# The second head mixing: 112 keys per product on two 64-row halves of the array, in place of 64 and 56 keys on its four quarters

## The chip, the cores and the metric

The kernel runs on one core of a Trainium2 chip. The metric is the device time of one execution in microseconds (us); shorter is better. A core has five engines with queues of their own: TensorE (PE; its weight loads are shown apart as PEld), VectorE (DVE), ScalarE (ACT), GpSimd (POOL) and SyncE (SP, which here only issues DMA transfers). TensorE writes to PSUM, from where ACT and DVE copy results to SBUF.

## The reference

Attention with heads mixed twice ("talking heads"), followed by an MLP with a SiLU, all in float32; batch 4, 12 heads, 448 positions, head width 64, model width 768, hidden width 2048.

```
scores = scale * q @ k^T                          # per batch and head
scores = einsum('bhij,hg->bgij', scores, w_pre)   # first mixing over heads
attn   = softmax(scores)                          # over the keys j
attn   = einsum('bhij,hg->bgij', attn, w_post)    # second mixing over heads
x      = attn @ v                                 # values, then heads side by side
h      = x @ w_in;  g = h * sigmoid(h);  out = g @ w_out
```

## The kernel before

**Two phases.** Up to about 440 us the kernel does the attention; the MLP products (line 624) fill the rest. While the attention runs, the MLP's weights come from float64 words, are converted on DVE, ACT and POOL (lines 63 to 93) and are written back to HBM, so those engines and the DMA queues are shared.

**Groups.** Each batch's 448 query rows are cut into four tiles of 100 to 120 rows. A tile is cut into groups of 10 query rows. A group lies in SBUF as two halves of 64 partitions, each with 60 used rows (5 query rows of 12 heads, row after row), so that mixing over heads is a product with a block-diagonal 60 by 60 matrix on one half of the array. There are 184 groups, worked on in 92 pairs, and the loop over groups takes one pair in two iterations.

**One pair.** `scores` (line 339) makes q k^T for two heads side by side, one on each 64-row half of the array. The copies of it (`st`, lines 344 and 346) are sent by DMA (line 351, SP's queue) into the group layout `g`. `mix_pair` (line 399) does the first mixing of a pair, DVE takes the row maximum (`nm`, line 405), ACT the exponential and its sum (`e`, line 409), POOL and DVE turn the sums into reciprocals (lines 418, 422), and POOL scales the mixing matrix by them (`wr`, line 425). `mix_pair_again` (line 437) is the second mixing. `put_pair` (line 446) copies its result from PSUM (`pa`, one buffer of two banks) to the tile `at` on ACT, and `values` (line 368) multiplies `at` by `v`, for two heads on two 64-column halves of the array. Transposes of q, k (lines 310, 269) stand between them.

**The second mixing in detail.** The exponentials are the stationary operand and `wr` (60 columns) the moving one, so that keys come out on the partitions. The 448 keys are four chunks (`j`) of 112. Each chunk and each row half `s` is cut into a key half `c`: 64 columns of weights for c=0 (56 keys, and 8 more that only fill), 56 for c=1. So the array is used as four 64 by 64 quarters, in the order (0,0), (1,1), (0,1), (1,0), and each quarter writes its own 64 partitions of PSUM; row half `s` has a PSUM bank of its own. A pair is 32 products; a float32 product is issued as two loads of weights and two matrix instructions, so the trace shows 64 of each.

**The values' rows.** `at` and the values have the same gap: 120 partitions, of which rows 56 to 63 are filler. `load_v_quad` (line 251) loads four heads of v in two transfers of 56 rows each (line 259), and where the tile held something else before (the same four tiles serve as space for k, line 240), GpSimd first zeroes rows 32 to 63 (line 256).

**What sets the order.** Each engine takes its instructions in the order in which the program emits them; there is no planner. In an even iteration the loop emits `mix_pair` of a later pair, then the work laid on that iteration in the order prep_q, prep_k, values, scores, then `mix_pair_again`; in an odd iteration such work alone. SP's queue holds the transfers of v, k, q, `st` and the MLP weights in one line. Six `scores` steps for the next tile lie on six successive iterations.

Of the kernel before, what the change touches and what calls it, by code (L numbers as in the profile page):

```python
# [8 lines left out]
F32 = mybir.dt.float32  # L9
# [94 lines left out]
def talking_heads_then_silu_mlp(  # L104
# [11 lines left out]
    nc = tc.nc  # L116
    ctx.enter_context(tc.manual_schedule())
    B, H, S, D = q.shape
# [3 lines left out]
    RH = R // 2  # L122
    GP = 128
    HP = GP // 2
    GH = RH * H
    G0 = HP - GH
    JT = 112
    NJ = S // JT
    JH = JT // 2
    KV = 64 + JH  # L130
    HH = H // 2
    TQ = 12 * R
    LEAD = 4
# [34 lines left out]
    def pool(name, bufs, stack=ctx, **kw):  # L168
        return stack.enter_context(tc.tile_pool(name=name, bufs=bufs, **kw))
# [5 lines left out]
    v2_p = pool("v2", 4, late, side="right")  # L175
    a_p = pool("a", 2, late, side="right")
# [16 lines left out]
    pa = ps_a.tile([128, 2, 512], F32, name="pa", tag="pa")  # L193
    turns = []

    def bank(p, name):
        if p is ps_a:
            turns.append(name)
            return pa[:, len(turns) % 2]
        return p.tile([128, 512], F32, name=name, tag="bank")  # L200

    v_tiles = [v2_p.tile([KV, 4, NJ, D], F32, name="v4", tag="v4") for _ in range(4)]
    zeroed = []
    g_tiles = [p.tile([GP, 12, S], F32, name="g", tag="g") for p in g_ps]

    def load_weights():
# [31 lines left out]
    def load_k_pair(b, h, queues=(nc.sync, nc.sync)):  # L238
        if h >= 4 if b == 0 else h // 4 != 1:
            x = (b * H + 8) // 4 % 4 if b else h // 4 - 1  # L240
            if x in zeroed:
                zeroed.remove(x)
            t = v_tiles[x][:JT, h % 4:h % 4 + 2].rearrange("p i j d -> p (i j d)")
            t = t.rearrange("p (j i d) -> p j i d", i=2, j=NJ)
        else:
            t = nat.tile([JT, NJ, 2, D], F32, name="kn", tag="kn")
        kns[b, h] = t
        for i in range(2):
            queues[i].dma_start(out=t[:, :, i, :], in_=k[b, h + i].rearrange("(p j) d -> p j d", p=JT))

    def load_v_quad(b, h):
        x = (b * H + h + 8) // 4 % 4
        t = v_tiles[x]
        if x not in zeroed:
            zeroed.append(x)
            nc.gpsimd.memset(t[32:64], 0.0)
        src = v[b, h:h + 4].rearrange("i (c p j) d -> c p i j d", c=2, p=JH)
        for c in (1, 0):
            nc.sync.dma_start(out=t[64 * c:64 * c + JH], in_=src[c])
        for i in range(0, 4, 2):  # L260
            vs[b, h + i] = t[:, i:i + 2]

# [117 lines left out]
    class Group:  # L380
# [48 lines left out]
        def mix_pair_again(self, other):  # L429

            for x, g in enumerate((self, other)):
                half = pa[:, :, x * 256:x * 256 + NJ * GH]
                for j in range(NJ):
                    for s, c in ((0, 0), (1, 1), (0, 1), (1, 0)):
                        rows = slice(HP * s, HP * (s + 1))
                        m = JH if c else 64
                        nc.tensor.matmul(  # L437
                            half[64 * c:64 * c + m, s, j * GH:(j + 1) * GH],
                            lhsT=g.e[rows, j * JT + c * JH:j * JT + c * JH + m], rhs=g.wr[rows], start=True, stop=True)

        def put_pair(self):
            if self.slot == 0:
                ats[self.n] = a_p.tile([KV, NJ, H, TQ], F32, name="at", tag="at")
            o, np, p = self.place()
            o += 2 * p * R
            nc.scalar.copy(  # L446
                out=ats[self.n].rearrange("p j g t -> p (j g) t")[:, :, o:o + 2 * R].rearrange("p x (c i) -> p x c i", i=RH),
                in_=pa[:KV].rearrange("p s (g w) -> p (s g) w", g=2)[:, :, :NJ * GH].rearrange("p c (x i) -> p x c i", i=RH))

    seq = [(b, ti) for b in range(B) for ti in range(len(tiles))]  # L450
    kns, qns, ks, vs, qs, gs, ats = {}, {}, {}, {}, {}, {}, {}
# [9 lines left out]
    at = lambda i: groups[i] if 0 <= i < len(groups) else None  # L461
# [13 lines left out]
    for n in range(1, len(seq)):  # L475
        p0, p1 = first[n - 1], first[n]
        spread = (0, 0, 0, 0, 2, 2) if n == 1 else (-6, -5, -4, -2, -1, 0) if p1 - p0 == 12 else (-6, -5, -4, -3, -2, -1)
        for h in range(0 if n > 1 else 2 * NE, H, 2):
            i = p0 + spread[h // 2]
# [7 lines left out]
    for n, (b, ti) in enumerate(seq):  # L487
        if n:
            p0 = first[n - 1]
            if n > 2:  # L490
                put(first[n - 2], lambda n=n: load_q(n)[0](), lead=7, w=2.1)
            for hg, i in ((0, p0 - 9), (1, p0 - 8)):
                if n > 1:
                    put(i, prep_q, n, hg)
            if ti == 0:
                c0 = first[n - 2]
                for h, i, lead in zip(range(0, H, 2), (0, 1, 3, 5, 7, 9), (10, 10, 11, 12, 5, 6)):
                    put(c0 + i, load_k_pair, b, h, lead=lead, w=1.2)
                    put(c0 + i, prep_k, b, h)
        if ti == 0:  # L500
            for h in range(0, H, 4):
                put(first[n] + ((5, 6, 8) if n else (15, 16, 18))[h // 4], load_v_quad, b, h, lead=2, w=1.8)
# [23 lines left out]
    for h in range(0, 6, 2):  # L526
        load_k_pair(0, h, (nc.sync, nc.scalar))
    loads[1]()
    for h in range(6, H, 2):
        load_k_pair(0, h)  # L530
# [58 lines left out]
    for j in range(WB, len(parts)):  # L589
        kind, m = ("i", "o")[j // (7 * NP)], j // NP % 7  # L590
        kind0, m0, p0 = ("i", "o")[(j - WB) // (7 * NP)], (j - WB) // NP % 7, (j - WB) % NP
        n = HC if kind0 == "i" else HF
        s = step_of[kind0, m0, NU - 1, (4 * p0 + 3) // n] + 1
        s = max(s, step_of[kind, m, 0, 0] - (10 if kind == "i" or m == 0 else 3))
# [52 lines left out]
    for kind, n, nk, blocks in (("i", HF, HC, xs), ("o", HC, HF, gr)):  # L647
        for m in range(7):
            for u in range(NU):
                s = step_of[kind, m, u, 0]  # L650
# [5 lines left out]
        for d, (x, y, z) in enumerate(DIFFER):  # L656
            for u in range(NU):
                s = step_of[kind, d, u, 0] if kind == "o" or d > 1 else step_of[kind, 0, u, 0]
# [8 lines left out]
    for i in range(len(groups) + 1):  # L667
        g, new, old = at(i), at(i + LEAD), at(i - 1)
# [182 lines left out]
    for s, (kind, m, u, a) in enumerate(steps):  # L851
# [14 lines left out]
        p = None  # L866
        if s >= len(phs):
            p = bank(ps_h, "ph")
# [58 lines left out]
```

## Time and profile before

| | |
|---|---|
| median of 3 runs | 872.0 us (870.98, 872.0, 878.78) |
| the profiled execution | 876.44 us, span 874.7 us from the first to the last instruction |
| mean granted TensorE clock | 0.977 of full speed |
| TensorE, matrix instructions | 828.4 us busy, 11058 instructions |
| TensorE, weight loads | 656.0 us, 11058 instructions |
| DVE, ACT, POOL | 625.4, 526.5, 406.4 us busy |

Busy time of an engine counts each moment once, though instructions overlap; a matrix instruction's duration holds its way through the array, so that neighbours overlap in time. Lines are written L437 for line 437. In the chain of waits, the work that ended last is followed back from the last instruction to whatever released it, so each microsecond of the span is put down to one line. "Idle before" in square brackets is the time for which the engine stood still ahead of the row, and what ended it. Shapes such as 64*56 are rows by columns of the array in use.

### The profile page before, as it was taken

What the parts mean: (1) busy time and instruction counts of PE and PEld (TensorE: products, weight loads), DVE (VectorE), ACT (ScalarE), POOL (GpSimd) and SP (SyncE); (2) the same over time, 40 slices, a digit from 0 to 9 for tenths busy, and PEclk for the clock granted to TensorE, in tenths of its full rate; (3) what the DMA queues carried; (4) which work ended last, traced back from release to release, by engine and by line L of the source; (5) the groups of instructions that cost most, each with busy time, mean ns of one, the idle gap of its engine ahead of it and who ended that gap; (6) DMA issues with size and microseconds to landing.
All of it is one profiled execution on the core that took longest, in us unless ns stands there. A gap on an engine that the chain in (4) does not pass through costs nothing.

```text
span 874.7 us, 27490 instructions
## 1 busy us (share of the span) xinstructions
PE 828.4 (95%) x11058; PEld 656.0 (75%) x11058; DVE 625.4 (71%) x1218; ACT 526.5 (60%) x1178; POOL 406.4 (46%) x681
## 2 busy tenths in 40 slices
PE   7797999899998999899899999999999999999997
PEld 5355666567666666666599999988899889999986
DVE  5453777468775777675878899999988689984332
ACT  4575778578786878677756653324694245343242
POOL 6231445355454645463877577557742233133020
PEclk7999899899999999999999999999999999999999
DMA  7569677887788787874635453355331142112234
GB/s 143 167 182 193 185 212 218 219 216 196 209 242 229 220 219 211 228 214 151 188 104 184 144 167 118 118 151 155 107 94 49 35 114 71 38 49 73 73 85 106
DMA packets 162343, 132.89 MB, mean 152 GB/s; under 512 B 50409, under 2 KB 155861, under 8 KB 162215
## 3 DMA queue, kind: packets, MB, share of 16 engines
q1 hardware_dynamic: 158809, 129.39, 53.0%
q8 instruction: 87, 1.43, 0.7%
q0 software_dynamic: 544, 1.03, 0.5%
q10 hardware_dynamic: 2862, 0.71, 0.4%
q14 instruction: 41, 0.34, 0.1%
HBM read 64.01 MB, written 27.53 MB: 105 GB/s over the span
## 4 chain that ended last, share of the span: by engine, by line
PE 75%; DVE 9%; DMA 7%; ACT 4%; issue 2%; SPq 2%; POOL 1%; ACTq 0%; POOLq 0%; DVEq 0%
PE ph L624 41%; PE pa L437 8%; PE pp L399 8%; PE po L368 7%; PE pqk L339 7%; DMA g<-st 4%; ACT e L409 2%; DVE nm L405 1%; DVE g L824 1%; PE pt L269 1%; PE ptt L844 1%; ACT at L446 1%; DVE op L630 1%; DMA v<-in_v 1%; DVE cg L92 1%
## 5 line engine op out<-in xcount | busy, mean ns | idle before, releaser
L624 PE MATMUL ph<-op,wh 128*128 128x448 f32 x924 | 221.5, 368 | 2.4 <-DVE g L834 1.8
L610 POOL TENSOR_TENSOR wl<-wl,wh 128x512 fp32r<-128x512 f32 x84 | 122.0, 1467 | 152.8 <-ACT wh L609 152.3
L624 PEld LDWEIGHTS ph<-op,wh 128*128 128x128 f32 x924 | 171.6, 188 | 18.1 <-DVE g L834 2.1
L405 DVE TENSOR_REDUCE nm<-pp 128x1 f32<-128x448 f32 x184 | 106.1, 618 | 76.1 <-PE pp L399 75.7
L425 POOL TENSOR_SCALAR wr<-wpost,r 128x60 f32<-128x60 f32 x184 | 70.7, 397 | 177.5 <-DVE r L422 139.0
L409 ACT ACTIVATE e<-pp,nm 128x448 f32<-128x448 f32 x184 | 115.4, 631 | 51.1 <-DVE nm L405 48.8
L437 PEld LDWEIGHTS pa<-wr,e 64*64 64x64 f32 (+1 forms) x5888 | 96.7, 131 | 44.9 <-issue 26.5
L437 PE MATMUL pa<-wr,e 64*64 64x60 f32 (+1 forms) x5888 | 108.6, 219 | 14.4 <-ACT at L446 8.6
L624 PE MATMUL ph<-op,wl 128*128 128x448 f32 x462 | 118.9, 366 | 0.0
L399 PE MATMUL pp<-g,wpre 64*64 64x448 f32 x736 | 104.9, 591 | 9.6 <-ACT e L409 5.7
L66 POOL TENSOR_TENSOR cg<-cw,cg 128x256 f32<-128x256 f32 x96 | 75.8, 790 | 76.6 <-DVE cw L63 73.5
L624 PEld LDWEIGHTS ph<-op,wl 128*128 128x128 f32 x462 | 86.7, 188 | 7.5 <-POOL wl L610 0.5
L446 ACT COPY at<-pa 120x960 f32<-120x960 f32 x92 | 89.9, 978 | 3.2 <-PE pa L437 3.2
L368 PE MATMUL po<-at,v 120*64 120x120 f32 (+1 forms) x1536 | 88.1, 268 | 1.8 <-DMA v<-in_v 1.5
L368 PEld LDWEIGHTS po<-at,v 120*64 120x64 f32 x1536 | 77.4, 139 | 14.6 <-issue 5.1
L609 ACT CAST wh<-wl 128x512 fp32r<-128x512 f32 x84 | 51.1, 617 | 54.3 <-DMA wl<-wo_dram 27.2
L344 DVE COPY st<-pqk 120x448 f32<-120x448 f32 (+1 forms) x89 | 55.0, 618 | 36.5 <-PE pqk L339 17.5
L90 ACT ACTIVATE cg<-cg,ebias 128x256 int32<-128x256 int32 x96 | 49.6, 516 | 44.2 <-DVE cg L86 43.0
L92 DVE SCALAR_TENSOR_TENSOR cg<-cw,cg 128x256 int32<-128x256 int32 x96 | 56.2, 586 | 16.4 <-ACT cg L90 16.0
L624 PE MATMUL ph<-x,wh 128*128 128x448 f32 x252 | 64.7, 365 | 0.0
L339 PEld LDWEIGHTS pqk<-kh,qh 64*120 64x120 f32 (+1 forms) x186 | 19.0, 179 | 50.0 <-issue 17.7
L339 PE MATMUL pqk<-kh,qh 64*120 64x448 f32 (+1 forms) x186 | 47.6, 467 | 6.8 <-ACT st L346 5.4
(122 smaller groups left out, 1379.0 us busy)
## 6 DMA issues: line engine op xcount, KB each, us to landing
g<-st SPq DMA_DIRECT2D x132, 210.0 KB
cw<-in_moe_w_in SPq DMA_DIRECT2D x48, 256.0 KB
cw<-in_moe_w_out SPq DMA_DIRECT2D x48, 256.0 KB
wi_dram<-cg SPq DMA_DIRECT2D x24, 448.0 KB
wo_dram<-cg SPq DMA_DIRECT2D x24, 448.0 KB
wl<-wi_dram SPq DMA_DIRECT2D x42, 256.0 KB
wl<-wo_dram SPq DMA_DIRECT2D x42, 256.0 KB
g<-st SPq DMA_DIRECT2D x48, 175.0 KB
```

Of the source, the lines that this page charges most:

```text
L66: nc.gpsimd.tensor_mul(out=e, in0=m, in1=e)
L92: nc.vector.scalar_tensor_tensor(out=e, in0=hi, scalar=-2 ** 31, in1=e, op0=ALU.bitwise_and, op1=ALU.bitwise_or)
L339: nc.tensor.matmul(ps[i][:m, :S], lhsT=q_[rows, hh, :m], rhs=k_[rows], start=(step == 0), stop=(step == 2))
L368: nc.tensor.matmul(po[i * D:(i + 1) * D, c * m:(c + 1) * m], lhsT=vs[b, h][:, i, j, :], rhs=ats[n][:, j, h + i, :m], start=(j == 0), stop= ...
L399: nc.tensor.matmul((self, other)[r].p[HP * c:HP * (c + 1), :S], lhsT=wpre[rows], rhs=gs[self.n][rows, o // R + c * np + p, :], start=True, ...
L405: nc.vector.tensor_reduce(out=self.nm, in_=self.p[:GP, :S], axis=AX.X, op=ALU.max, negate=True)
L409: nc.scalar.activation(out=self.e, in_=self.p[:GP, :S], func=AF.Exp, bias=self.nm, scale=1.0, accum_out=sums)
L425: nc.gpsimd.tensor_scalar(out=g.wr, in0=wpost.rearrange("p g i -> p (g i)"), scalar1=r[:, i:i + 1], scalar2=1.0, op0=ALU.mult, op1=ALU.mult)
L437: nc.tensor.matmul(half[64 * c:64 * c + m, s, j * GH:(j + 1) * GH], lhsT=g.e[rows, j * JT + c * JH:j * JT + c * JH + m], rhs=g.wr[rows], s ...
L446: nc.scalar.copy(out=ats[self.n].rearrange("p j g t -> p (j g) t")[:, :, o:o + 2 * R].rearrange("p x (c i) -> p x c i", i=RH), in_=pa[:KV] ...
L610: nc.gpsimd.tensor_sub(out=wl, in0=raw(wl), in1=raw(wh))
L624: nc.tensor.matmul(p[:, :T], lhsT=w, rhs=x, start=(n == 0), stop=(n == len(todo) - 1))
```

## The change

`mix_pair_again` no longer cuts a chunk of 112 keys in two: each row half takes all 112 as one stationary operand, so that the array is used as two halves of 64 rows by 128 columns, and a pair is 16 products (32 loads and 32 matrix instructions). With that the gap in `at` and in the values goes: both are 112 partitions, v comes in one transfer of 112 rows per four heads (12 transfers, not 24), and the zeroing on GpSimd and the list that records it are taken out. The order of keys, the moving operand, the copy's free shape and the order of the steps are as before.

```diff
-    v_tiles = [v2_p.tile([KV, 4, NJ, D], F32, name="v4", tag="v4") for _ in range(4)]
-    zeroed = []
+    v_tiles = [v2_p.tile([JT, 4, NJ, D], F32, name="v4", tag="v4") for _ in range(4)]
...
-        if x not in zeroed:
-            zeroed.append(x)
-            nc.gpsimd.memset(t[32:64], 0.0)
-        src = v[b, h:h + 4].rearrange("i (c p j) d -> c p i j d", c=2, p=JH)
-        for c in (1, 0):
-            nc.sync.dma_start(out=t[64 * c:64 * c + JH], in_=src[c])
+        nc.sync.dma_start(out=t, in_=v[b, h:h + 4].rearrange("i (p j) d -> p i j d", p=JT))
...
                 for j in range(NJ):
-                    for s, c in ((0, 0), (1, 1), (0, 1), (1, 0)):
+                    for s in range(2):
                         rows = slice(HP * s, HP * (s + 1))
-                        m = JH if c else 64
                         nc.tensor.matmul(
-                            half[64 * c:64 * c + m, s, j * GH:(j + 1) * GH],
-                            lhsT=g.e[rows, j * JT + c * JH:j * JT + c * JH + m], rhs=g.wr[rows], start=True, stop=True)
+                            half[:JT, s, j * GH:(j + 1) * GH], lhsT=g.e[rows, j * JT:(j + 1) * JT], rhs=g.wr[rows],
+                            start=True, stop=True)
...
-                ats[self.n] = a_p.tile([KV, NJ, H, TQ], F32, name="at", tag="at")
+                ats[self.n] = a_p.tile([JT, NJ, H, TQ], F32, name="at", tag="at")
...
-                in_=pa[:KV].rearrange("p s (g w) -> p (s g) w", g=2)[:, :, :NJ * GH].rearrange("p c (x i) -> p x c i", i=RH))
+                in_=pa[:JT].rearrange("p s (g w) -> p (s g) w", g=2)[:, :, :NJ * GH].rearrange("p c (x i) -> p x c i", i=RH))
```

## Rows read from the trace of the kernel before

**Rows 1.** The page's busy time: engine, us (share of the span), instructions.
```profile
PE 828.4 (95%) x11058; PEld 656.0 (75%) x11058; DVE 625.4 (71%) x1218; ACT 526.5 (60%) x1178; POOL 406.4 (46%) x681
```

**Rows 2.** Windows: from:to, length, busy (count) per engine, clock, DMA share, GB/s.
```profile
34.00:438.00 404.00, 375.25 (x8707) 250.25 (x8706) 270.58 (x644) 306.75 (x742) 192.88 (x454) 0.97 0.75 206
...
18.00:24.80 6.80, 5.41 (x42) 3.44 (x38) 4.54 (x10) 4.71 (x8) 6.80 (x7) 1.00 0.58 158
...
300.00:312.00 12.00, 11.54 (x240) 8.06 (x239) 9.17 (x22) 10.11 (x24) 6.16 (x16) 1.00 0.93 239
```

**Rows 3.** Chain of waits: shares of the span by line, then pieces (start, us, what).
```profile
by line: PE ph L624 41.4%; PE pa L437 8.2%; PE pp L399 7.6%; PE po L368 7.2%; PE pqk L339 6.9%; DMA g<-st 3.9%; issue 2.1%; ACT e L409 1.5%; DVE nm L405 1.4%; DVE g L824 1.3%; PE pt L269 1.3%; PE ptt L844 1.0%; ACT at L446 1.0%; DVE op L630
...
117.49 1.09 PE pa L437 x58
...
159.97 9.64 DMA g<-st
```

**Rows 4.** Timeline, 300 to 312 us: start, us, engine, line, operation, count [idle before].
```profile
301.28 1.63 PEld L368 LDWEIGHTS po<-at,v 120*64 120x64 f32 x32 [0.70 <-ACT kh L274]
301.28 1.86 PE L368 MATMUL po<-at,v 120*64 120x120 f32 x32
...
303.07 1.02 PEld L437 LDWEIGHTS pa<-wr,e 64*64 64x64 f32 x64 [0.16 <-issue]
303.07 1.16 PE L437 MATMUL pa<-wr,e 64*64 64x60 f32 x64
...
304.16 0.53 PE L310 MATMUL pt<-ident,qn 120*128 120x120 f32 x3
...
304.52 0.55 PE L269 MATMUL pt<-ident,kn 112*128 112x112 f32 x4
...
305.00 0.98 PE L399 MATMUL pp<-g,wpre 64*64 64x448 f32 x8
...
306.91 1.16 PE L437 MATMUL pa<-wr,e 64*64 64x60 f32 x64 [0.46 <-ACT at L446]
```

**Rows 5.** Groups by line and form: count | busy us, mean ns | idle before.
```profile
L437 PE MATMUL pa<-wr,e 64*64 64x60 f32 x2944 | 108.6, 222 | 14.2 <-ACT at L446 8.6 <-issue 3.4 <-POOL cg L66 1.3
...
L437 PE MATMUL pa<-wr,e 64*56 64x60 f32 x2944 | 98.7, 217 | 0.2 <-issue 0.2
...
L437 PEld LDWEIGHTS pa<-wr,e 64*64 64x64 f32 x2944 | 96.7, 135 | 44.9 <-issue 26.5 <-POOL r L418 5.2 <-POOL cg L66 4.3
...
L437 PEld LDWEIGHTS pa<-wr,e 64*56 64x56 f32 x2944 | 86.0, 127 | 0.0
```

**Rows 6.** Timeline, 18 to 25 us: weight loads, then matrix instructions.
```profile
18.14 0.18 PEld L339 LDWEIGHTS pqk<-kl,qh 64*120 64x120 f32 x2
18.34 0.18 PEld L339 LDWEIGHTS pqk<-kh,qh 64*120 64x120 f32 x2
...
24.05 0.52 PEld L516 LDWEIGHTS pa<-ident 128*128 128x128 f32 x4 [0.32 <-DVE st L344]
...
18.14 0.36 PE L339 MATMUL pqk<-kh,ql 64*120 64x448 f32 x2
18.34 0.37 PE L339 MATMUL pqk<-kl,qh 64*120 64x448 f32 x2
```

**Rows 7.** Timeline of TensorE, 52 to 58 us: what stands beside the second mixing.
```profile
52.56 1.16 PE L437 MATMUL pa<-wr,e 64*64 64x60 f32 x64
53.53 1.42 PE L399 MATMUL pp<-g,wpre 64*64 64x448 f32 x8
...
55.19 0.37 PE L339 MATMUL pqk<-kh,ql 64*120 64x448 f32 x2
55.39 0.37 PE L339 MATMUL pqk<-kl,qh 64*120 64x448 f32 x2
55.69 1.16 PE L437 MATMUL pa<-wr,e 64*64 64x60 f32 x64
56.78 0.46 PE L339 MATMUL pqk<-kh,qh 64*120 64x448 f32 x2
```

**Rows 8.** The values' line: each operation's count and ns (min/median/max), first and last start.
```profile
L259 SPq DMA_DIRECT2D v<-in_v x24: 316/594/4061, 61.0 to 361.7; - x24
L256 POOL MEMSET v<- x6: 942/942/946, 60.9 to 352.4; 32x1024 f32 x6
```

**Rows 9.** Waits of SP's queue, 34 to 440 us: us in total, times, longest.
```profile
SPq L259 <- POOL r L418: 5.5, 5, 1.8
```

**Rows 10.** Timeline, 60 to 92 us: a stall of TensorE in the first batch.
```profile
87.89 0.69 PE L339 MATMUL pqk<-kh,qh 64*100 64x448 f32 x1 [4.54 <-ACT st L346]
```

More of the change, by code (lines that the diff above doesn't have):

```diff
@@ L128, in talking_heads_then_silu_mlp @@
     NJ = S // JT
-    JH = JT // 2
-    KV = 64 + JH
     HH = H // 2
@@ L240, in load_k_pair @@
             x = (b * H + 8) // 4 % 4 if b else h // 4 - 1
-            if x in zeroed:
-                zeroed.remove(x)
-            t = v_tiles[x][:JT, h % 4:h % 4 + 2].rearrange("p i j d -> p (i j d)")
+            t = v_tiles[x][:, h % 4:h % 4 + 2].rearrange("p i j d -> p (i j d)")
             t = t.rearrange("p (j i d) -> p j i d", i=2, j=NJ)
```

## Prediction

> **What bounds the kernel now.** I read the busy times first: TensorE's matrix instructions fill 95% of the span, DVE, the next engine, 71% [rows 1]. That is a hint only, since their durations overlap; so next I read the attention phase as a window, because the change touches nothing after it. There TensorE is busy 375.25 of 404 us at a mean clock of 0.97, ACT 306.75, DVE 270.58 [rows 2]. TensorE stands still for 28.75 us in all, and that is the slack that could hide longer work. Third, the chain of waits: the second mixing (L437) alone holds 8.2% of the span, 0.082 x 874.7 = 71.7 us; a whole burst of it stands on the chain with 1.09 us [rows 3], so some 71.7 / 1.09 = 66 of the 92 bursts lie on the path that sets the end. Fourth, the timeline of one iteration shows why: values, second mixing, transposes and first mixing follow on TensorE with no gap between them (301.28 to 305.98 us), and the next burst waits only 0.46 us, for the copy L446, which itself waited in ACT's queue behind work fed by TensorE [rows 4]. Whatever lengthens a burst there lengthens the iteration.
>
> **What sets the pace of a burst.** This is the step on which all hangs. A burst has 64 loads of weights in 1.02 us [rows 4]; four quarters work side by side, so each does 16 in a row. The loads of 64 and of 56 columns occur equally often with the same 60 moving columns, and yet those of 64 take 96.7 us together and those of 56 take 86.0 [rows 5]: a ratio of 1.124, against 64/56 = 1.143. So the columns loaded set the pace of the 64-column quarters, not the moving columns, and not the count. One round (one load on every quarter) takes (1.02 - 0.14) / 15 = 0.0587 us, with 0.14 for the last load's own duration. The only row with full-width loads at full clock and a short moving operand is the 128-column product of L516: four loads in 0.52 us, each about 0.19, so (0.52 - 0.19) / 3 = 0.110 us a round [rows 6]. Both stretches had the clock of 1.00 of full speed, that is 2.4 GHz [rows 2]. The straight line through 64 and 128 columns gives 0.0008 us per column, and for 112 columns 0.0587 + 48 x 0.0008 = 0.0971 us.
>
> Do two 64-row loads run side by side? In the scores, which use the array just as the change will (64 rows, 120 columns), two loads together take the 0.18 us that one takes, and the matrix instructions of two successive steps begin 0.20 us apart though their 448 columns alone are most of that [rows 6]; so the halves load at once, and a load hides under the matrix instruction ahead of it.
>
> **The change part by part.** *The burst.* Sixteen rounds stay sixteen: four chunks, two groups, two instructions a product. Before, a round was four loads of at most 64 columns; now it is two of 112. Half the instructions go, no round goes, and each becomes 0.0971 - 0.0587 = 0.0384 us longer: 16 x 0.0384 = 0.614 us per burst, from 1.09 to about 1.70 us. The bounds are the nearest rows: 0.0587 (a round stays as it is, +0) and 0.110 (a 128-column round, 16 x 0.0513 = +0.82 us). I take the value between, since 112 lies nearer to 128. The trace of the scores shows the 120-column load with 0.18 us against 0.135 for 64 columns [rows 5, 6], the same slope. The Trainium skill ("TensorE: Matmul & The Clock Gate", section LDWEIGHTS) says that a load takes its columns divided by 1.2 GHz, whatever the rows; by that a round would go from 53 to 93 ns, a burst would grow by 0.64 us and the first term below would be 42 us, so the rule speaks against this change as the rows do.
>
> On the chain: 66 x 0.614 = +40.5 us. The 26 other bursts grow by 16 us in all, where TensorE waits for something else, as in the stalls of 4.54 us for a copy [rows 10] and 9.64 us for a transfer [rows 3]. Their cover is the 28.75 us of idle time; but only idle time right behind a burst helps, so I count a quarter, +4 (bounds 0 and +16).
>
> *The array's shape at a burst's edges.* From the second to the first mixing, both on quarters, the next instruction starts 0.97 us after the burst's start; where scores follow, 1.09: 0.12 us is paid for the change of shape. Ahead of a burst, scores to scores take 0.20 us and scores to burst 0.30 [rows 7]. Now the burst has the scores' shape: edges with scores get up to 0.10 us cheaper, edges with the first mixing up to 0.12 dearer; others stay. By the order of emission scores stand right ahead of the burst in about half of the pairs, 45 of 92, and behind it in fewer. Bounds: 90 x 0.10 = -9, and 47 x 0.12 = +6; I take -4.
>
> *Loads of v and the zeroing.* Six zeroings of 0.94 us go from POOL, and 12 of 24 issues, median 0.594 us, from SP; the bytes stay [rows 8]. POOL is 46% busy [rows 1], so its 5.7 us buy little by themselves. On SP's one line a v transfer that waits for POOL holds up the scores' transfers behind it: 5.5 us in five waits [rows 9]. If all of that were cover for nothing else, -6; if the waits are for a reader of the tile and stay, 0; a doubled transfer that lands later for the values is excluded as a loss beyond 2 us, since values need both parts anyhow. I take -2.
>
> *At no cost.* The ACT copy keeps its 960 elements per partition, the values keep their 64 columns loaded and 120 moved; 112 rows instead of 120 change neither count [rows 4]. If row count mattered, it would be a gain of at most a fifteenth of either.
>
> *The sum.* 40.5 + 4 - 4 - 2 = +38.5 us. Against the profiled execution that is 876.4 + 38.5 = 914.9; that execution stands 4.4 us above the median of the runs, 872.0, so I forecast 910 us.
>
> **The rivals.** *A, faster: the number of instructions sets the pace.* Place: the 128 instructions of a burst at TensorE's front end. A load and matrix pair starts every 1.02 / 64 = 0.016 us; if that were the limit, 32 pairs would take half, the burst would fall by 0.5 us, the chain by 66 x 0.5 = 33, and with -6 for the edges and v the time would be 833. It decides if two wide loads cost less than four narrow ones, that is if a round stays under 0.0587. For it: half the instructions do go. Against it: the 64-column loads are slower than the 56-column ones at equal counts [rows 5]. The Trainium skill ("TensorEngine Tiling (Array Packing)", section Instruction Overhead) gives each matmul about 60 cycles of overhead, by which the moving 60 columns would be at the floor and the count would rule, as in this rival; the trace does not agree, as 64 matrix instructions in 1.16 us are 18 ns each. Chance 0.07.
>
> *B, the slack takes most of it.* If the 28.75 us of idle time lie right behind bursts, 16 + 40.5 - 28.75 = +28, and with the shape and v at their best ends (-9 and -6) +13: 885. For it: stalls do occur in the attention; against: they follow transfers and copies that TensorE's own earlier scores feed, so they move along. Chance 0.08 for 880 to 893.
>
> *C, a round stays 0.0587.* Then nothing but the edges and v remain: -6, 866, within 1%. For it: the lower bound of the burst; against it: L516's 0.110. Chance 0.05.
>
> *D, the loads stop hiding.* If in the new shape a load waits for its half's matrix instruction, a round is 0.0971 plus some 0.05 for the 60 moving columns (half of the 0.10 that 120 take in the values: 1.63 / 32 x 2 halves [rows 4]): +0.0384 + 0.05 = 0.088 x 16 = 1.41 us, 66 times: +93, 959. Against it: the scores' 0.20 us spacing [rows 6]. Chance 0.04.
>
> **How the numbers follow.** The forecast, 893 to 930, has chance 0.76: its lower end is the sum with v and edges at -15 and no help lost off the chain (+26), its upper end all 92 bursts at 0.614 (56) plus 2. The range reaches down to B's lower part, 885, and up to 930; that holds 0.8. What a measurement of this kernel can tell from no change is about 1%, 863 to 881: C's place. Faster 0.07 (A), within 1% 0.06 (C and the edge of B), slower 0.87.
>
> **What would show it.** In the changed trace: bursts of L437 with 32 loads in about 1.5 us and 1.6 to 1.7 us on the chain; loads of 112 columns near 0.175 us each; L437's share of the chain near 112 of 915 us; starts of burst and scores 0.1 us closer. Wrong: 32 loads in 0.5 us (A) or 1.0 (C) or 2.3 (D); or bursts that grow while TensorE's idle time in the attention falls by as much (B).

## The result: slower by 1.4%, a third of the forecast

The changed kernel takes 889.27 us (median of 6 runs, 883.32 to 890.92) where the kernel before, in the same session, takes 877.66 (870.98 to 887.74): ratio 1.0138, 95% interval 1.01 to 1.0175, which is +12 us. Two more sets of runs of the changed kernel gave 1.0155 (1.01 to 1.021) and 1.0148 (1.0103 to 1.0193). Forecast were +38 us and 910 us: the right sign, three times the size. The profiled execution took 885.52 us, with a span of 883.8.

The page of the changed kernel, busy times and the queue that brings instructions (packets, MB, share). The lines have moved by about ten: the second mixing is L426, its copy L435, first mixing L389, scores L329, values L358.

```profile
PE 856.3 (97%) x8114; PEld 708.8 (80%) x8114; DVE 625.1 (71%) x1218; ACT 527.8 (60%) x1178; POOL 401.5 (45%) x675
...
q8 instruction: 64, 1.05, 0.5%
```

Its timeline around one burst (compare [rows 4]), TensorE's loads and matrix instructions:

```profile
302.49 1.65 PEld L426 LDWEIGHTS pa<-wr,e 64*112 64x112 f32 x32 [0.16 <-issue]
...
302.49 1.79 PE L426 MATMUL pa<-wr,e 64*112 64x60 f32 x32
304.21 0.53 PE L300 MATMUL pt<-ident,qn 120*128 120x120 f32 x3
```

The burst did what was forecast: 16 rounds in 1.65 us, of which the last load is 0.175 (the mean of these loads on the page is 175 ns), so (1.65 - 0.175) / 15 = 0.098 us a round against a forecast of 0.0971. From the burst's start to the next instruction it takes 1.72 us (before 1.09). At the scores it is less, as this timeline of the changed kernel shows (compare [rows 7]):

```profile
50.60 0.37 PE L329 MATMUL pqk<-kl,qh 64*120 64x448 f32 x2
50.80 1.69 PE L426 MATMUL pa<-wr,e 64*112 64x60 f32 x32
52.42 0.98 PE L389 MATMUL pp<-g,wpre 64*64 64x448 f32 x8
...
54.05 1.69 PE L426 MATMUL pa<-wr,e 64*112 64x60 f32 x32
55.55 0.45 PE L329 MATMUL pqk<-kh,qh 64*120 64x448 f32 x2
```

Scores to burst take 0.20 us (before 0.30), burst to scores 1.50, burst to first mixing 1.62: the 0.12 us for a change of shape has gone over from one neighbour to the other.

So the cost came; something else gave most of it back. The windows of the changed kernel show where, with busy times per engine, the granted clock and the DMA share:

```profile
34.00:438.00 404.00, 392.93 (x5626) 294.11 (x5625) 264.30 (x633) 300.96 (x724) 181.51 (x437) 1.00 0.73 202
...
68.00:100.00 32.00, 30.67 (x440) 23.08 (x438) 18.59 (x44) 22.45 (x55) 9.61 (x25) 1.00 0.90 222
...
140.00:180.00 40.00, 39.23 (x594) 29.70 (x592) 25.96 (x66) 30.07 (x75) 18.69 (x47) 1.00 0.85 215
```

And the last two for the kernel before, with a short piece inside each:

```profile
68.00:100.00 32.00, 27.18 (x547) 17.98 (x547) 14.31 (x35) 18.50 (x46) 6.93 (x19) 0.89 0.84 190
140.00:180.00 40.00, 35.06 (x793) 22.72 (x789) 23.96 (x59) 27.83 (x66) 18.28 (x43) 0.91 0.84 226
...
88.00:92.00 4.00, 4.00 (x19) 1.65 (x19) 2.34 (x6) 1.96 (x5) 0.74 (x1) 0.50 0.78 211
...
172.00:175.00 3.00, 3.00 (x18) 1.28 (x19) 1.51 (x4) 1.71 (x5) 0.49 (x2) 0.50 0.64 230
```

TensorE's idle time in the attention fell from 28.75 us [rows 2] to 404 - 392.93 = 11.07. And its clock stands at full speed for longer. In the kernel before it was at half (1.2 GHz) around the stalls (0.50 from 88 to 92 and from 172 to 175 us), which makes 0.89 and 0.91 of these two stretches. From the first burst to the last, the trace of the kernel before has 23.9 us at half clock, in 20.7 of which TensorE worked; that of the changed kernel has 3.4, with 3.3 of work. A burst and a first mixing in such a piece of the kernel before, right behind waits for the scores' copies:

```profile
168.13 1.94 PE L437 MATMUL pa<-wr,e 64*64 64x60 f32 x64
171.72 2.38 PE L399 MATMUL pp<-g,wpre 64*64 64x448 f32 x8 [1.65 <-ACT e L409]
```

They take 1.94 and 2.38 us where [rows 4] have 1.16 and 0.98. Which waits went is read from TensorE's waits in 34 to 438 us (us in total, times, longest). Before:

```profile
PE pa L437 <- ACT at L446: 8.6, 17, 1.1
PE pp L399 <- ACT e L409: 5.7, 6, 1.7
PE pqk L339 <- ACT st L346: 5.4, 2, 4.5
PE pa L437 <- issue: 3.6, 3, 2.0
PE po L368 <- DMA v<-in_v: 1.5, 1, 1.5
PE pqk L339 <- DVE st L344: 1.4, 2, 1.1
PE pa L437 <- POOL cg L66: 1.3, 1, 1.3
...
PE po L368 <- issue: 0.3, 1, 0.3
```

After, in full:

```profile
PE pa L426 <- ACT at L435: 7.8, 18, 1.1
PE pt L300 <- ACT st L336: 1.2, 1, 1.2
PE pqk L329 <- ACT st L336: 0.9, 1, 0.9
PE pa L426 <- POOL cg L71: 0.6, 1, 0.6
```

The wait for the burst's own copy stays; the waits for exponentials, for the scores' copies, for v and for nothing visible ("issue") nearly vanish. The chain of waits of the changed kernel says the same (compare [rows 3]):

```profile
by line: PE ph L613 39.4%; PE pa L426 14.5%; PE po L358 8.3%; PE pp L389 7.6%; PE pqk L329 7.3%; DMA g<-st 1.6%; issue 1.6%; SPq L244 1.3%; ACT at L435 1.3%; DVE g L813 1.3%; PE ptt L833 1.0%; DVE op L619 1.0%; DVE g L815 1.0%; DVE cg L92 1
```

The second mixing's part grew from 71.7 to 0.145 x 883.8 = 128 us, the scores' transfers fell from 34 to 14.

**The account.** From the first burst to the last instruction of the last one, TensorE's time can be cut at the start of each group of like instructions, idle time apart. Summed from the two traces, in us, before to after: second mixing 101.8 to 151.0 (+49.2), scores 74.1 to 65.0 (-9.1), first mixing 94.0 to 85.4 (-8.6), values 80.7 to 78.3 (-2.4), transposes 23.2 to 22.8 (-0.4), idle 28.7 to 11.5 (-17.2): +11.5 in all. Of the -20.5 us of the four middle terms, some 6 are edges: about 60 of them, from scores to a burst, at 0.10 us. Some 8 are clock, if work at half clock takes twice its time (18.9 us of work outside the bursts stood at half clock before, 3.3 after). The other 6 or 7 are neither. Most of that is in the first mixing: 12 of them took over 1.0 us at full clock in the kernel before (1.42 us at 53.53 in [rows 7]), 4 in the changed kernel, where 0.91 is usual. These are probably short waits for the exponentials, hidden under the recorded durations; no run shows it apart. (The span grew by 9.1 us. The first burst began at 29.8 us and not at 34.2, before anything that the change touches, as it did in some of the quarter kernels below; behind the last burst the changed kernel took 2 us more.)

One profile of each kernel is compared here. In the two other profiles of the changed kernel (taken with experiments 2 and 5) the same sum is +14.6 and +15.6 us, the idle time 13.0 and 14.3 us, and the time at half clock 10.2 us in each, so single terms are good to 3 or 4 us.

### The profile page after: what moved, and what is told of

It is laid out like the page before. It is cut to its first block, busy times and chain, and to the rows that moved or that the text cites. A ratio compares the mean times of both kernels' runs of the same rounds, so it can differ in the third digit from the quotient of the medians.

```text
span 883.8 us, 21565 instructions
## 1 busy us (share of the span) xinstructions
PE 856.3 (97%) x8114; PEld 708.8 (80%) x8114; DVE 625.1 (71%) x1218; ACT 527.8 (60%) x1178; POOL 401.5 (45%) x675
## 4 chain that ended last, share of the span: by engine, by line
PE 80%; DVE 9%; ACT 3%; DMA 3%; SPq 2%; issue 2%; POOL 0%; ACTq 0%; DVEq 0%; POOLq 0%
PE ph L613 39%; PE pa L426 14%; PE po L358 8%; PE pp L389 8%; PE pqk L329 7%; DMA g<-st 2%; SPq L244 1%; ACT at L435 1%; DVE g L813 1%; PE ptt L833 1%; DVE op L619 1%; DVE g L815 1%; DVE cg L92 1%; PE pt L259 1%; ACT e L399 1%
## 5 line engine op out<-in xcount | busy, mean ns | idle before, releaser
L426 PEld LDWEIGHTS pa<-wr,e 64*112 64x112 f32 x2944 | 157.4, 175 | 25.9 <-issue 12.0
L426 PE MATMUL pa<-wr,e 64*112 64x60 f32 x2944 | 160.6, 258 | 9.1 <-ACT at L435 8.2
L389 PE MATMUL pp<-g,wpre 64*64 64x448 f32 x736 | 95.3, 571 | 0.8 <-ACT e L399 0.5
L435 ACT COPY at<-pa 112x960 f32<-112x960 f32 x92 | 89.6, 974 | 5.8 <-PE pa L426 5.8
L358 PE MATMUL po<-at,v 112*64 112x120 f32 (+1 forms) x1536 | 85.7, 265 | 0.0
L358 PEld LDWEIGHTS po<-at,v 112*64 112x64 f32 x1536 | 75.5, 137 | 11.0 <-issue 5.2
L329 PEld LDWEIGHTS pqk<-kh,qh 64*120 64x120 f32 (+1 forms) x186 | 18.8, 176 | 40.9 <-issue 21.5
L336 ACT COPY st<-pqk 120x448 f32<-120x448 f32 (+1 forms) x89 | 47.9, 539 | 4.2 <-DMA g<-st 3.1
```

Of the source, the lines that this page charges most:

```text
L329: nc.tensor.matmul(ps[i][:m, :S], lhsT=q_[rows, hh, :m], rhs=k_[rows], start=(step == 0), stop=(step == 2))
L358: nc.tensor.matmul(po[i * D:(i + 1) * D, c * m:(c + 1) * m], lhsT=vs[b, h][:, i, j, :], rhs=ats[n][:, j, h + i, :m], start=(j == 0), stop= ...
L389: nc.tensor.matmul((self, other)[r].p[HP * c:HP * (c + 1), :S], lhsT=wpre[rows], rhs=gs[self.n][rows, o // R + c * np + p, :], start=True, ...
L426: nc.tensor.matmul(half[:JT, s, j * GH:(j + 1) * GH], lhsT=g.e[rows, j * JT:(j + 1) * JT], rhs=g.wr[rows], start=True, stop=True)
L435: nc.scalar.copy(out=ats[self.n].rearrange("p j g t -> p (j g) t")[:, :, o:o + 2 * R].rearrange("p x (c i) -> p x c i", i=RH), in_=pa[:JT] ...
```

## Experiments

Each kernel was timed in five rounds against the kernel before. Theory S: longer bursts take the place of idle and slow-clock time that TensorE had anyway. Theory V: the new loads of v removed the stalls. Theory I, formed after experiments 1 to 3: half the instructions relieve TensorE's supply of instructions.

**1. The new loads of v alone.** On top of the changed kernel, the mixing goes back to quarters, cut so that no gap is needed:

```diff
-                    for s in range(2):
+                    for s, c in ((0, 0), (1, 1), (0, 1), (1, 0)):
...
+                        m = JT - 64 if c else 64
...
+                            half[64 * c:64 * c + m, s, j * GH:(j + 1) * GH],
+                            lhsT=g.e[rows, j * JT + c * 64:j * JT + c * 64 + m], rhs=g.wr[rows], start=True, stop=True)
```

> The new loads of v (112 rows, one transfer, no zeroing) with the mixing back on four quarters, cut into 64 and 48 keys, so that there is no gap either. The round should stay at 0.0587 us, as the 64-column quarters set it, and the burst at 1.09 us. Theory V (the new loads of v took TensorE's stalls away, and the wide loads cost what was forecast): 15 to 25 us faster than the kernel before, some 855 to 862 us, with TensorE's idle time in the attention near 10 us. Theory S (the longer bursts filled idle time that was there anyway, and v matters little): within 5 us of the kernel before, idle time of TensorE in the attention still 20 to 30 us.

Measured: ratio 0.9985 (0.9953 to 1.0017), TensorE idle for 404 - 375.07 = 28.9 us in 34 to 438 us:

```profile
34.00:438.00 404.00, 375.07 (x8696) 251.87 (x8689) 269.42 (x643) 306.47 (x739) 188.65 (x449) 0.97 0.75 207
```

TensorE stands still as long as in the kernel before, though not for the same waits alone (more for "issue", see experiment 3). Theory V falls: v's transfers and the zeroing are worth nothing that can be told from zero on the quarters.

**2. The wide mixing with the old loads of v.** The changed kernel with two transfers of 56 rows and a zeroing:

```diff
...
-        nc.sync.dma_start(out=t, in_=v[b, h:h + 4].rearrange("i (p j) d -> p i j d", p=JT))
+        if x not in zeroed:
+            zeroed.append(x)
+            nc.gpsimd.memset(t[32:56], 0.0)
+        src = v[b, h:h + 4].rearrange("i (c p j) d -> c p i j d", c=2, p=JT // 2)
+        for c in (1, 0):
+            nc.sync.dma_start(out=t[56 * c:56 * c + 56], in_=src[c])
```

> The changed kernel's mixing on two halves with v loaded as before: two transfers of 56 rows per quad, and a zeroing on GpSimd (24 rows, at the same places in the order) that the second transfer waits for. Theory V: 15 to 25 us slower than the changed kernel, 900 to 912 us, with stalls of TensorE back. Theory S: within 4 us of the changed kernel (889 us), idle time of TensorE in the attention 9 to 14 us.

Measured: 1.0205 (1.0147 to 1.0263), idle 404 - 391.43 = 12.6 us:

```profile
34.00:438.00 404.00, 391.43 (x5489) 292.45 (x5486) 256.39 (x612) 294.29 (x707) 178.73 (x427) 0.98 0.72 196
```

It was run again beside the changed kernel:

> The changed kernel's mixing with the old loads of v once more, now beside the changed kernel on the same chip. If the loads of v matter (theory V, in a small form): 4 to 8 us slower than the changed kernel beside it. If not: within 3 us of it.

> The changed kernel, as the yardstick for the run with the old loads of v: 1.010 to 1.018 of the kernel before.

Measured: 1.0181 (1.0134 to 1.0229) against 1.0148 (1.0103 to 1.0193), medians 893.50 and 887.53 us. The idle time stays low with the old loads too. The loads of v may be worth 3 to 6 us on the halves, but the intervals overlap; the forecast's -2 us is neither shown nor refuted.

**3. Longer bursts on the quarters, with more instructions.** The kernel before mixes two of the four chunks twice (8 more rounds), or one (4 more, with `(0,)`):

```diff
-                for j in range(NJ):
+                for j in (*range(NJ), *(0, 1)):
```

> The kernel before with chunks 0 and 1 of every group mixed twice (the same values written again): 8 more rounds on four quarters, 8 x 0.0587 = 0.47 us per burst and 43 us in all, close to the 45.5 us by which the bursts grew in the changed kernel; loads of v and the array's shape as before. Theory S: the same fate as the change, +12 to +22 us (no cheaper edges beside the scores), TensorE's idle time in the attention down from 29 to 10 to 15 us and its mean clock there up to 1.00. Theory V: +35 to +43 us, the stalls still there.

> The kernel before with chunk 0 of every group mixed twice: 4 more rounds, 0.235 us per burst, 21.6 us in all. Theory S: most of it goes into idle time and into the clock, 0 to +8 us, so that the second 21.6 us (the run with 8 more rounds) cost more than the first. Theory V, or any theory in which TensorE's time on the chain simply adds: +15 to +21 us, half of the run with 8 more rounds.

Measured: 1.0578 (1.0503 to 1.0654) for 8 rounds, +51 us; 1.0306 (1.0264 to 1.0347) for 4, +27 us. Both above the TensorE time added (43 and 21.6), where theory S wanted a third of it, and with 8 rounds TensorE's idle time in 34 to 438 us rose, to 404 - 370.07 = 33.9 us. The trace of the kernel with 8 more rounds shows a wait that is rare before. Its timeline of TensorE:

```profile
193.05 0.47 PE L368 MATMUL po<-at,v 120*64 120x120 f32 x5
195.33 0.88 PE L368 MATMUL po<-at,v 120*64 120x120 f32 x13 [1.81 <-issue]
196.14 0.98 PE L399 MATMUL pp<-g,wpre 64*64 64x448 f32 x8
197.05 0.45 PE L339 MATMUL pqk<-kh,qh 64*100 64x448 f32 x2
197.34 0.36 PE L339 MATMUL pqk<-kh,ql 64*100 64x448 f32 x2
197.54 0.37 PE L339 MATMUL pqk<-kl,qh 64*100 64x448 f32 x2
197.83 1.62 PE L437 MATMUL pa<-wr,e 64*64 64x60 f32 x96
199.39 0.45 PE L339 MATMUL pqk<-kh,qh 64*100 64x448 f32 x2
199.67 0.37 PE L339 MATMUL pqk<-kh,ql 64*100 64x448 f32 x2
202.63 0.44 PE L339 MATMUL pqk<-kl,qh 64*100 64x448 f32 x2 [2.59 <-issue]
```

TensorE stops in the middle of `values` and in the middle of a step of the scores, where no other engine is waited for, and between the two stops lie 13 + 8 + 2 + 2 + 2 + 96 + 2 + 2 = 127 matrix instructions, with their loads 254. The page's instruction queue has for this kernel

```profile
q8 instruction: 110, 1.80, 0.9%
```

so a packet carries 1.80 MB / 110 = 16.4 KB, and 2 x 14002 instructions of TensorE over 110 packets make 255 each. The stops stand one packet apart: TensorE had used up its instructions and waited for the next packet. In this kernel's trace the stops of over 0.6 us from 130 to 400 us, 15 of them, all stand at the same place of a packet (counted in the instructions of TensorE's queue, its waits on semaphores included, the remainder by 256 is 193 or 194), and each ends 1.3 to 1.7 us after a packet's transfer ended. The waits put down to "issue", kernel with 8 more rounds:

```profile
PE pa L437 <- issue: 10.4, 9, 3.8
PE pqk L339 <- issue: 9.0, 6, 2.6
PE po L368 <- issue: 5.5, 3, 2.7
PE pt L310 <- issue: 0.9, 1, 0.9
PE pp L399 <- issue: 0.2, 1, 0.2
```

That is 26.0 us (21.6 with 4 more rounds, 3.9 in the kernel before, 10.4 and 9.0 in the quarter kernels of experiments 1 and 6, 7.0, 5.0 and 1.8 in those of experiment 4 with 141, 282 and 448 columns, none in any profile of the mixing with 112 columns).

**4. Longer bursts with few instructions.** To part the time from the instructions, four products with many moving columns stand ahead of each burst of the kernel before, written to the same PSUM tile and overwritten by it:

```diff
+            for s, c in ((0, 0), (1, 1), (0, 1), (1, 0)):
+                rows = slice(HP * s, HP * (s + 1))
+                nc.tensor.matmul(
+                    pa[HP * c:HP * (c + 1), s, :282], lhsT=wpre[rows], rhs=self.e[rows, :282], start=True, stop=True)
```

> The kernel before with 4 more products ahead of every burst, on the four quarters and into the same PSUM tile (overwritten by the burst): 282 moving columns, so 2 rounds of 0.235 us, 0.47 us per burst and 43 us in all, the TensorE time of the run with 8 more rounds, but with 16 instructions more per pair instead of 64. Theory S (idle time and clock take up longer bursts wherever they come from; the 8 more rounds cost so much only because TensorE ran out of instructions): +12 to +22 us, idle time in the attention near 11 us, clock near 1.00. Theory A (TensorE's time adds in full on the quarters): +40 to +50 us. Between them: the share of the shape's edges and of the instructions.

> The same with 141 moving columns: 0.235 us per burst, 21.6 us in all. Theory S: 0 to +8 us, less than half of the run with 282 columns, since the first microseconds go into idle time. Theory A: +20 to +25 us, half of that run.

> The kernel before with the 4 extra products of 448 moving columns: 0.373 us a round, 0.747 us per burst, 69 us in all. Theory S (idle time and lost clock are a store of some 25 us that longer bursts use up): the first 43 us cost 18, the next 26 should cost nearly all of their length, +38 to +45 us. If instead every us of TensorE's time costs 0.42 us throughout: +29 us.

Measured: 1.0205 (1.0142 to 1.0268) for 43 us of TensorE time, 1.0105 (1.0042 to 1.0167) for 21.6, 1.0346 (1.0312 to 1.0379) for 69: +18, +9 and +30 us. This parts the two: with the same added time as the 8 rounds, but a quarter of their added instructions, the cost is 18 us and not 51. In the profiles of these two kernels (8 more rounds, 282 columns) the spans differ by 27.1 us, and TensorE's idle time from the first burst to the last by 21.6 (40.2 against 18.6). Theory S holds in its main claim, on quarters and with the old loads of v. The waits of the kernel with 448 columns, 34 to 438 us, in full:

```profile
PE pa L433 <- ACT at L450: 4.1, 13, 0.4
PE pqk L339 <- ACT st L346: 3.4, 1, 3.4
PE po L368 <- issue: 1.3, 2, 0.7
PE pqk L339 <- DVE st L344: 1.0, 1, 1.0
PE pa L441 <- issue: 0.5, 1, 0.5
PE pp L399 <- ACT e L409: 0.2, 1, 0.2
```

10.5 us in all, where the kernel before has 28.3 (13.8 in 28 to 471 us, which takes in all bursts of this kernel). But the store does not run dry as theory S had it: 69 us cost 30, below the 38 to 45 foreseen and near the 29 of the other case, so by the times a microsecond of TensorE costs about 0.43 over this whole range. The one profile is less clear: from the first burst to the last the attention took 37.3 us more than in the kernel before, and the first burst began 5.4 us sooner, ahead of anything that the edit touches.

**5. The wide mixing with twice the instructions.** The changed kernel loads 52 columns twice instead of 112 once (one over the other; keys and columns beyond 52 are left out):

```diff
...
+                        pieces = [(s, 56 * c, 52, 52) for s, c in ((0, 0), (1, 0), (0, 1), (1, 1))]
...
+                            half[:m, s, j * GH:j * GH + w], lhsT=g.e[rows, j * JT + o:j * JT + o + m],
+                            rhs=g.wr[rows, :w], start=True, stop=True)
```

> The changed kernel with every chunk mixed in two loads of 52 columns with 52 moving ones on the same two halves, one over the other (all but the first pair; it leaves out the other keys and columns). A round should take 2 x 52 + 12 cycles or 0.0483 us, so 32 rounds 1.55 us, the time of 16 rounds of 0.0976 us, at the same shape and with the instruction count of the kernel before (64 loads and 64 matrix instructions a burst). Theory I (the halved instruction count is what gave the time back): 12 us or more slower than the changed kernel, 900 us or more, with gaps of 1 to 3 us at TensorE that end 1.3 to 1.6 us after a block of instructions has landed. Theory S: within 4 us of the changed kernel.

> The changed kernel unchanged, as the yardstick for the runs of this call and for the run with the old loads of v: all theories say 1.010 to 1.018 of the kernel before, 886 to 891 us.

Measured: 1.0276 (1.0214 to 1.0339) beside 1.0155 (1.01 to 1.021), medians 900.49 and 890.17 us: 10 us slower, near theory I's 12, but not for its reason. The trace of the kernel with 52 columns:

```profile
203.33 1.62 PEld L430 LDWEIGHTS pa<-wr,e 64*52 64x52 f32 x64 [0.16 <-issue]
...
213.18 0.37 PE L329 MATMUL pqk<-kl,qh 64*120 64x448 f32 x2
213.47 1.70 PE L430 MATMUL pa<-wr,e 64*52 64x52 f32 x62
```

The burst is as long as meant (1.62 us), but scores to burst takes 0.29 us again: with 52 columns the edges are those of the quarters. Summed as in the account, against the changed kernel timed beside it, the scores cost 7.7 us more and the burst 3.0; waits for "issue" are 3.6 us. The run shows the price of the edges better than that of the instructions.

**6. A shorter burst on the quarters.** In the kernel before, both key halves load 56 columns:

```diff
-                        m = JH if c else 64
+                        m = JH if c or self.n or self.slot else 64
```

> The kernel before with 56 weight columns for both key halves (all but the first pair, which fills the gap's rows once; the gap stays and is multiplied by the values' zero rows). The quarters that loaded 64 columns then pace themselves as those with 56 do: a round of 0.0525 us instead of 0.0584, a burst 0.09 us shorter, 8.5 us of TensorE's time in all. If TensorE's time counts at the 0.42 us per us of the runs with 141 and 282 moving columns: -3 to -4 us. If it counts in full: -8 us. If faster bursts only run into the supply of instructions: 0.

Measured: 0.9978 (0.9947 to 1.001), not clear of no change. The burst fell as foreseen: its timeline has

```profile
303.17 1.06 PE L437 MATMUL pa<-wr,e 64*56 64x60 f32 x64
```

against 1.16 us in [rows 4]. The waits for "issue" rose to 9.0 us in its profile. No version tried beats the kernel before beyond doubt.

## Why the prediction was wrong

- **Pace of a burst: right.** 0.098 us a round against 0.0971; rivals A, C and D fall with it. That the columns loaded set it, experiment 6 bears out (56 for 64 columns: 1.06 for 1.16 us). All bursts together cost TensorE 49.2 us more with the edge behind them, some 43 with the edge ahead as well; the steps gave 92 x 0.614 - 4 = 52.5 with both edges.
- **The failed step: "On the chain: 66 x 0.614 = +40.5 us", and with it the quarter taken for the rest.** It holds only if every other piece of the chain keeps its length. The pieces between the bursts do not: waits for transfers and copies are over, or shorter, when TensorE comes later. Against the 49.2 us of the bursts stand 17.2 us less idle time, some 8 of clock, some 6 of edges and 6 or 7 of hidden waits, which leaves +11.5; the steps let waits take 12, all from bursts off the chain, and nothing else but 4 of edges and 2 of v. Rival B, at 0.08, was the nearest case, and what I held against it (that the stalls move along with TensorE's own scores) is refuted by experiment 4: with TensorE time added ahead of each burst and nothing else changed, the waits fell from 28.3 to 10.5 us.
- **A term left out: the clock.** Its mean in the attention went from 0.97 to 1.00. Work at half clock fell from 20.7 to 3.3 us, which gives back (20.7 - 3.3) / 2 = some 9 us, 4 of them in the first mixing (10.0 us at half clock before, 2.1 after); this is an estimate that takes all work to pace with the clock. The prediction quotes the 0.97 of [rows 2] and puts no price on it. Four of the five slow stretches in the kernel before begin in a wait of TensorE or shortly behind one (of 4.54, 1.13, 1.68 and 1.98 us), so a stall can cost twice, once itself and once in the slow piece behind it. It need not: the kernel with 8 more rounds idles 40.2 us and has 17.1 at half clock, where the kernel before has 28.7 and 23.9.
- **A term left out: instructions.** The kernel before waits 3.9 us for them in its profile, the changed one not at all. That is a small share of what came back. Rival A had the front end's rate in mind, which no run shows as a limit; the limit that they show is the supply in packets.
- **Edges: right mechanism, size too small.** Scores fell by 9.1 us, some 6 of it at about 60 edges (the prediction counted 45), beside what the burst's own edge gave; forecast was -4 in all.
- **v and zeroing: -2 forecast;** within what the runs can't tell. TensorE's 1.5 us wait for v is gone in the changed kernel, but not in the quarter kernel with the same loads, which waits 1.3 us.
- **No cost for the copy and the values: right** (the copy: 978 ns each before, 974 after; the values' matrix instructions: 268 ns each and 88.1 us busy before, 265 ns and 85.7 us after).
- **A slip in the range.** The lower end, 893, does not come out of its terms: 872.0 + 40.5 - 15 is 897.5. The measured 889.27 us lies below both. That the wider range, from 885 on, holds it is owed to its having been stretched over part of rival B, not to the forecast's mechanism.

What stays open: why the transfers for the next tile are late in the kernel before at all; that SP's queue paces them, not TensorE, is argued and not tried. Why a microsecond of TensorE costs 0.43 even at 69 added. And whether the early start of the first burst in several profiles is chance.

## What to carry to other kernels

An engine that is 93% busy on the path that ends last still had 29 us of waits and some 10 us of slow clock to give, so a lengthened step cost a quarter of its length here, 0.43 in a plain test; scale the sum by such a test, and read the chain as where time went, not as what each microsecond is worth. Small products are priced by the columns they load, and by how many instructions they take from the supply: between kernels of equal TensorE time the instruction count made 33 us of difference (experiments 3 and 4).

## What the runs showed of the hardware

- Instructions come to TensorE in packets of 16.4 KB, about 255 loads and matrix instructions. At 64 pairs in 1.02 us the supply begins to fall behind: waits of 4 to 10 us in all with 128 instructions per burst, 22 with 160, 26 with 192. With 144 spread over a longer time (experiment 4) they are 2 to 7, with 128 in 1.62 us (experiment 5) 3.6, with 64 none: the pace at which instructions are used up counts, not their number alone.
- A round of 64-row float32 loads lasts 0.0587 us for 64 columns, 0.098 for 112, 0.110 for 128 with 128 rows: the columns count, and two or four parts of the array load side by side (four loads of 64 columns take little more than half as long as one of 128).
- Going from one division of the array to another costs about 0.1 us (from scores to burst 0.30 us, and 0.20 where the division stays), while the change from float32r to float32 at that edge costs nothing; a load of 52 columns has the edges of a 64-column part (0.29 us from scores to burst). The Trainium skill ("TensorEngine Tiling (Array Packing)", section Tiling Modes) says that a change of mode drains the engine; the traces agree as far as 0.1 us more at each such edge goes, and do not show a drain apart.
